# A column maximum over partitions moved from GpSimd to TensorE and VectorE in a fused Fourier, soft-MoE and SwiGLU kernel

## The chip, the core and the metric

The kernel runs on one core of one Trainium2 chip. The metric is the device time of one execution in microseconds; the figure for the kernel before is the median of three runs. A TensorE clock of 1.00 in a profile is 2.4 GHz.

## The reference

The input x has 8 batches of 3072 positions and 256 channels. Three layers follow each other. The first takes a real Fourier transform along the positions, a complex linear map with bias, a soft threshold and the inverse transform. The second is a soft mixture of experts with 8 experts of 4 slots, where the softmax of the dispatch runs over all 8 x 3072 = 24576 tokens and that of the combination over the 32 slots:

```python
logits = x @ phi                                  # 24576 x 32
d = np.exp(logits - logits.max(0, keepdims=True))
d /= d.sum(0, keepdims=True) + 1e-09
slot_input = d.T @ x                              # then two matrices per expert
c = np.exp(logits - logits.max(1, keepdims=True))
c /= c.sum(1, keepdims=True) + 1e-09
x = c @ slot_out
```

The third is an RMS norm with a gated product (silu(xn @ w_gate) * (xn @ w_val)) @ w_out. The change concerns `logits.max(0)`, a maximum per slot over all tokens.

## The kernel before

**Phase 1** (`phase1`) is one main loop (L709) over `u` from 0 to 287: 8 batches, three thirds each, 12 steps `m` per third. A slot in this document is one such step, numbered from the start of the batch in which it runs. In each step `emit_M` issues three matmuls of the complex linear map into one of two psM banks; at fixed steps `emit_A` (first transform stage, L224), `emit_B` (second stage, L261), `emit_T` (transposes through psT or psA, L376) and `emit_L` (logits in the frequency domain, L388) put in their matmuls. The evacuations of what TensorE produced are not issued at once: `post(f, k, rank)` puts them k slots later, at the start of that slot, and lower ranks come first there. L386, for example, is ScalarE's copy that empties the bank of an `emit_T` one slot later (rank -1). `new_t()` hands out the banks psT and psA in turn; `emit_A` can take both of them, and L245 and L247 empty them on ScalarE.

Beside this runs a converter (L131) that turns double-precision weights into fp32 on VectorE, one step in 12 of the 36 slots of a batch, slot 12 among them. L155 is its product; for one of the weights ScalarE's L158 follows it.

**The softmax chain.** `chain(b)` (L407) does the softmax of batch b. For the batches 0 to 6 it is a list of steps, each with the slot of batch b + 1 in which it is issued (the tuples `at`, L611 and L612, the second for the batches 0 to 5; a step with a second number is issued behind the matmuls of its slot). The chain inverts the transform of the logits, which gives 96 partitions x 32 positions x 32 slots (tile `l`). `dmax` (L450) takes the maximum over the 32 positions of a partition into `mx` (96 x 32; `si` in the trace). What is left is the maximum over the 96 partitions. `dpar` (L459) does it on GpSimd with `partition_all_reduce`, which leaves the result on all 128 partitions in `mb`, and `dpre` (L456) does the same with the running maximum of the batch before. `dmn` (L472, or L474 in batch 0) puts `mb` and the old running maximum together on VectorE. `dal` (L483) and `alexp` (L496) make the factor by which older sums are scaled. `dsub` (L487, two halves) and `dexp` (L492) make the dispatch weights, which TensorE uses from slot 23 (`fa`, L536). For the combination `cmax` (L500) takes the row maximum, `csub` (L504) subtracts on VectorE, `cexp` (L508) is an exponential on ScalarE, then `csum` and `cmul` (L518). The result goes to DRAM: for batch 0 in four DMAs on GpSimd's queue (L523), for 1 to 6 in one on SP's queue (L525).

The last batch has a chain of its own, which is issued after the main loop and keeps the all-reduces (`dold` with `dpre`, and `dpar(64)`).

Each engine works through its queue in order. GpSimd's own work in this phase is a subtraction per half `emit_B` (L295), which makes the low part of a high-low pair for the next third. An all-reduce needs another function library on GpSimd than L295, and the queue holds a MODIFY_POOL_CONFIG in front of a change of library.

**Phase 2** (`phase2`) is the experts and the gated product, the rest of the span, and is not touched.

Of the kernel before, what the change touches and what calls it, by code (L numbers as in the profile page):

```python
# [6 lines left out]
F32 = mybir.dt.float32  # L7
# [3 lines left out]
ALU = mybir.AluOpType  # L11
AX = mybir.AxisListType
# [3 lines left out]
NB, N, C = 8, 3072, 256  # L16
# [152 lines left out]
def phase1(tc, x, w_r, w_i, b_r, b_i, phi, t_d, t_bf, t_ci, t_ai, t_af, t_id,  # L169
           ident, s_run, z_run, c_d, cv_args, mid):  # L170
    from contextlib import ExitStack
    nc = tc.nc
# [7 lines left out]
    sm_p, mn_p = P(st_c, "sm", 1), P(st_c, "mn", 2)  # L180
# [13 lines left out]
    mx = mid.si.rearrange("p h s -> p (h s)")  # L194
# [9 lines left out]
    xraw, asb, bounce, bin_t, xq, xs, x0, yy, yts, lfs, mns, mix = ({} for _ in range(12))  # L204
# [3 lines left out]
    def post(f, k=1, rank=1):  # L208

        if clock[0] is None:  # L210
            f()
        else:
            pend.setdefault(clock[0] + k, []).append((rank, len(pend), f))
# [158 lines left out]
    def new_t():  # L372
        turn[0] += 1
        return bank(*((psT, "psT"), (psA, "psA"))[turn[0] % 2])
# [26 lines left out]
    def bank(p, n):  # L401
        return p.tile([128, 512], F32, name=n)
# [4 lines left out]
    def chain(b):  # L407

        S = {}
# [39 lines left out]
            v = S["l", k0].rearrange("p (n s) -> p n s", s=32) if k1 - k0 == 16 else l3(k0, k1)  # L449
            nc.vector.tensor_reduce(out=mx[0:96, o:o + 32], in_=v.rearrange("p n s -> p s n"), axis=AX.X, op=ALU.max)  # L450

        def dpre():
            if b < NB - 1:
                S["mb"] = sm_p.tile([128, 96], F32, name="mb")
            if b:
                nc.gpsimd.partition_all_reduce(out_ap=S["mb"][:, 0:32], in_ap=mns[b - 1], channels=128, reduce_op=ReduceOp.max)  # L456

        def dpar(w):
            nc.gpsimd.partition_all_reduce(out_ap=S["mb"][:, 0:w], in_ap=mx[:, 0:w], channels=128, reduce_op=ReduceOp.max)  # L459

        def dold():
            S["mb"] = sm_p.tile([128, 96], F32, name="mb")
            nc.vector.tensor_copy(out=S["mb"][:, 64:96], in_=mns[b - 1])
            dpre()

        def dmn(w):
            mb = S["mb"][:, 0:32]
            mn = mn_p.tile([128, 32], F32, name="mn")
            if w == 64:
                nc.vector.tensor_reduce(out=mn, in_=S["mb"].rearrange("p (k s) -> p s k", k=3), axis=AX.X, op=ALU.max)  # L470
            elif b:
                nc.vector.tensor_tensor(out=mn, in0=mb, in1=mns[b - 1], op=ALU.max)  # L472
            else:
                nc.vector.tensor_copy(out=mn, in_=mb)  # L474
            mns[b] = S["mn"] = mn
            if w == 32:
                dal()
            S["d"] = ch_p.tile([128, 1024], F32, name="ch")[0:96]

        def dal():  # L480
            if b:
                S["al"] = sm_p.tile([128, 32], F32, name="al")
                nc.vector.tensor_tensor(out=S["al"], in0=mns.pop(b - 1), in1=S["mn"], op=ALU.subtract)  # L483
# [32 lines left out]
        def cmul(eng=nc.gpsimd):  # L516
            S["c"] = ch_p.tile([128, 1024], F32, name="ch")[0:96]
            eng.tensor_tensor(out=S["c"].rearrange("p (n s) -> p n s", s=32), in0=S["e"].rearrange("p (n s) -> p n s", s=32),  # L518
                                    in1=S["sc"].unsqueeze(2).to_broadcast([96, 32, 32]), op=ALU.mult)
            if b == 0:  # L520
                v = c_d[0].rearrange("a b -> (a b)").rearrange("(a t n s) -> a n t s", a=4, t=32, s=32)
                for a in range(4):
                    nc.gpsimd.dma_start(out=v[a], in_=S["c"][24 * a:24 * a + 24].rearrange("n (t s) -> n t s", s=32))  # L523
            elif b < NB - 1:
                nc.sync.dma_start(out=c_d[b], in_=S["c"])  # L525
            else:
                mid.put_c = lambda: nc.sync.dma_start(out=c_d[b], in_=S["c"])
# [54 lines left out]
        def slot(g0, g1, ps):  # L582
            if g0 == 0:
                S["sl"] = ps
            ps = S["sl"]
            for pg in range(g0, g1):
                yt = yts.pop((b, pg))
                for g in range(4):
                    o = 32 * (4 * pg + g)
                    nc.tensor.matmul(out=ps[32 * g:32 * g + 32, 0:256], lhsT=S["D"][:, o:o + 32], rhs=yt[:, g, :],  # L590
                                     start=(pg == 0), stop=(pg == 5))
# [15 lines left out]
        def L(f, *a):  # L607
            return lambda: f(*a)

        if b < NB - 1:  # L610
            at = (12, 6, 9, 10, 10, 10, 13, 13, 11, 15, 14, 18, 19, 20, 16, 16, 25, 30, 22, 22, 26, 26, 29, 30, 32, 33, 34, 35) if b == NB - 2 else \  # L611
                 (12, 7, 8, 9, 9, 10, 13, 13, 15, 16, 13, 14, 19, 20, 15, 16, 18, 28, 23, 23, 26, 27, 31, 28, 28, 33, 34, 35)  # L612
            steps = [(dpre,), (clear,), (L(binv, 0, 24), 1), (L(t1, 0, 32),), (L(ainv, 0), 2), (L(ainv, 1), 2), (L(dmax, 0, 32),),
                     (L(dpar, 32),), (cmax,), (L(csub, nc.vector),), (L(dmn, 32),), (L(dsub, 0, 16),), (L(dsub, 16, 32),),
                     (L(dexp, 0, 32),), (alexp,), (cexp,), (csum,), (L(cmul, nc.vector),), (L(fa, 0, 16), 2),
                     (L(fa, 16, 32), 2), (L(t2, 0, 16),), (L(t2, 16, 32),), (alT,), (L(fb, 0, 12), 1),
                     (L(fb, 12, 24), 1), (L(dT, 0, 6),), (lambda: slot(0, 6, new_t()), 1), (s_up,)]
            return [(a, *e) for a, e in zip(at, steps)]

        def tr(q, ri, k):  # L620
            return lambda: emit_T(b, q, ri, bank(*((psT, "psT"), (psM, "psM"), (psM, "psM"), (psA, "psA"), (psB, "psB"))[k]))

        return [clear, L(binv, 0, 16), tr(0, 0, 1), tr(0, 1, 3), tr(1, 0, 4), lambda: emit_L(b, 2), L(binv, 16, 24),
                L(t1, 0, 16), tr(1, 1, 2), tr(2, 0, 1), L(ainv, 0, (psB, "psB")), L(t1, 16, 32), dold,
                L(ainv, 1, (psA, "psA")), L(dmax, 0, 16), L(lcopy, 0), halved, tr(2, 1, 0), tr(3, 0, 2),
                L(dmax, 16, 32), L(lcopy, 1), L(dpar, 64), tr(3, 1, 1), st_i.close, L(mid.open, 2), tr(4, 0, 0), L(dmn, 64),
                L(dsub, 0, 16), L(dexp, 0, 16), tr(4, 1, 1), L(busy, 2), L(fa, 0, 16, (psB, "psB")), L(dsub, 16, 32),
                L(dexp, 16, 32), dal, L(t2, 0, 16), L(fa, 16, 32, (psA, "psA")), alexp, alT, L(t2, 16, 32),
# [72 lines left out]
    S = 12 * W  # L701
    late, back = {}, {1: [(0, 3)], 8: [(0, 4)], 13: [(0, 5)]}
    for b in range(1, NB):
        for q, k in enumerate((-13, -13, -11, -6, -2, 6) if b > 1 else (-16, -15, -13, -6, -2, 6)):
            back.setdefault(36 * b + k, []).append((b, q))
    last = chain(NB - 1)


    for u in range(S):  # L709
        w, m = divmod(u, 12)  # L710
        b, qq = divmod(w, 3)
        clock[0] = u
        if qq == 0 and m == 0 and 1 <= b:
            for k, f, *pe in chain(b - 1):
                late.setdefault((u + k, pe[0] if pe else 0), []).append(f)
# [13 lines left out]
        if u in (26, 28, 30, 32):  # L729
            p = slice(3 * u - 78, 3 * u - 72)  # L730
# [7 lines left out]
        if w >= 1 and m in (2, 4, 6, 10) and w <= W - 3:  # L738
            k = (2, 4, 6, 10).index(m)
# [7 lines left out]
        at = (3, 5, 7, 9) if w % 3 == 2 else (3, 5, 7, 9)  # L747
        if w + 1 < W and m in at:
            k = at.index(m)
# [552 lines left out]
```

## Time and profile before

| | kernel before |
|---|---|
| median of 3 runs | 1686.51 us (1684.47 to 1688.64) |
| the profiled execution | 1684.44 us, span 1682.7 us |
| TensorE matmul, share of the span | 98% (1648.2 us) |
| VectorE | 77% (1297.2 us) |
| ScalarE | 64% (1073.8 us) |
| GpSimd | 7% (124.5 us, 140 instructions) |
| mean granted TensorE clock | 0.994 |

The span runs from the first to the last instruction of the profiled execution. The busy share of TensorE is modelled from pipelined matmuls, so it says that work was under way, not that it ran at its peak. Where a table of windows shows TensorE less busy than the window is long, it waited; where PEclk is below 1.00, what it did took longer. "Idle before" and the brackets at the end of timeline rows give the wait in front of an instruction and what ended it; "issue" is a wait for nothing that the profile shows.

### The profile page before, as it was taken

The page shows a single profiled execution, that of the slowest core. Times are in us where ns is not written, and L with a number is a line of the kernel's source. Part 1 is how long each engine was busy: PE and PEld are TensorE (multiplying, and loading weights), DVE is VectorE, ACT ScalarE, POOL GpSimd, SP SyncE. Part 2 cuts the span into 40 slices and gives each one's busy share as a digit, 9 for nine tenths or more (in the row PEclk, how much of TensorE's full clock was granted, in tenths as well). Part 3 has the DMA queues.
Part 4 walks back from the last instruction along what each step waited for, and adds up shares of the span by engine and source line. Part 5 has one row for each costly group of instructions (what it writes and reads, how often), then busy time and mean ns, then how long its engine had stood idle before and what let it go on. Part 6 is the DMA issues. An engine that isn't in the chain of part 4 may idle for free.

```text
span 1682.7 us, 27265 instructions
## 1 busy us (share of the span) xinstructions
PE 1648.2 (98%) x10313; PEld 1312.9 (78%) x10313; DVE 1297.2 (77%) x2288; ACT 1073.8 (64%) x2078; POOL 124.5 (7%) x140
## 2 busy tenths in 40 slices
PE   8999999999999999999999999999999999999999
PEld 5667666676676568888888888888888888888887
DVE  3678878778688488878877877877877887887775
ACT  3767666666664376666666666666666666666664
POOL 0112111111111110000000000000000000000000
PEclk9999999999999999999999999999999999999999
DMA  8866666566553931200200110020021021020001
GB/s 307 306 218 194 204 196 209 176 207 215 177 185 123 326 106 39 69 29 26 64 24 24 52 47 26 26 72 26 13 64 35 26 64 35 26 63 13 26 26 38
DMA packets 107619, 172.52 MB, mean 103 GB/s; under 512 B 9248, under 2 KB 70912, under 8 KB 107488
## 3 DMA queue, kind: packets, MB, share of 16 engines
q1 hardware_dynamic: 106912, 169.97, 31.5%
q8 instruction: 81, 1.33, 0.3%
q0 software_dynamic: 432, 0.78, 0.3%
q14 instruction: 50, 0.41, 0.1%
q10 hardware_dynamic: 144, 0.03, 0.0%
HBM read 98.65 MB, written 59.77 MB: 94 GB/s over the span
## 4 chain that ended last, share of the span: by engine, by line
PE 91%; DVE 3%; issue 2%; ACT 2%; DMA 1%; POOL 0%; SPq 0%; ACTq 0%; POOLq 0%
PE po L1185 16%; PE pe L1185 16%; PE psM L319 10%; PE po L1186 8%; PE pe L1186 8%; PE pg L1157 8%; PE pv L1159 8%; PE psB L271 4%; PE psC L237 1%; PE psT L237 1%; PE psA L384 1%; PE psT L384 1%; PE psC L536 1%; PE psC L419 1%; PE psA L590 1%
## 5 line engine op out<-in xcount | busy, mean ns | idle before, releaser
L1163 DVE TENSOR_TENSOR h<-s,pv 128x512 f32<-128x512 f32 x576 | 394.8, 685 | 185.2 <-ACT s L1161 177.0
L1161 ACT ACTIVATE s<-pg 128x512 f32<-128x512 f32 x576 | 345.4, 600 | 296.9 <-PE pg L1157 295.5
L1185 PE MATMUL po<-wo,hh 128*128 128x512 f32 x1152 | 428.6, 396 | 0.0
L1185 PE MATMUL pe<-wo,hh 128*128 128x512 f32 x1152 | 423.9, 392 | 0.0
L107 DVE TENSOR_TENSOR hl<-h,hh 128x512 fp32r<-128x512 f32 x572 | 400.2, 700 | 0.1
L106 ACT ACTIVATE hh<-h 128x512 fp32r<-128x512 f32 x576 | 360.6, 626 | 1.4 <-DVE h L1163 1.2
L1186 PE MATMUL po<-wo,hl 128*128 128x256 f32 x1152 | 322.5, 280 | 0.0
L1186 PE MATMUL pe<-wo,hl 128*128 128x256 f32 x1152 | 322.0, 280 | 0.0
L1185 PEld LDWEIGHTS po<-wo,hh 128*128 128x128 f32 x1152 | 216.3, 188 | 50.9
L1185 PEld LDWEIGHTS pe<-wo,hh 128*128 128x128 f32 x1152 | 216.4, 188 | 49.7
L1186 PEld LDWEIGHTS pe<-wo,hl 128*128 128x128 f32 x1152 | 215.9, 187 | 22.9
L1157 PE MATMUL pg<-cq,gst 128*128 128x512 f32 x576 | 227.8, 396 | 0.7 <-ACT cq L1090 0.7
L1159 PE MATMUL pv<-cq,gst 128*128 128x512 f32 x576 | 227.0, 394 | 0.3 <-DVE h L1163 0.2
L1186 PEld LDWEIGHTS po<-wo,hl 128*128 128x128 f32 x1152 | 216.3, 188 | 2.7
L319 PE MATMUL psM<-xq,wh 128*128 128x512 f32 x384 | 169.8, 452 | 0.3 <-DVE yy L332 0.3
L1157 PEld LDWEIGHTS pg<-cq,gst 128*128 128x128 f32 x576 | 108.5, 188 | 25.1 <-ACT cq L1090 1.1
L271 PEld LDWEIGHTS psB<-bf,bin 128*128 128x128 f32 x752 | 98.8, 195 | 24.9 <-issue 13.9
L1159 PEld LDWEIGHTS pv<-cq,gst 128*128 128x128 f32 x576 | 109.0, 189 | 2.2 <-DVE h L1163 1.7
L295 POOL TENSOR_TENSOR xs<-xt,xs 128x256 fp32r<-128x256 f32 x92 | 78.2, 851 | 391.9 <-ACT xs L294 367.2
L271 PE MATMUL psB<-bf,bin 128*128 128x128 f32 x752 | 102.8, 281 | 4.3 <-DMA bin<-bounce 2.5
L319 PEld LDWEIGHTS psM<-xq,wh 128*128 128x128 f32 x384 | 73.7, 192 | 34.8 <-issue 24.2
L335 ACT ACTIVATE r<-yy,b_lo 128x512 f32<-128x512 f32 (+1 forms) x92 | 66.2, 720 | 27.5 <-DVE yy L338 27.3
(311 smaller groups left out, 1873.6 us busy)
## 6 DMA issues: line engine op xcount, KB each, us to landing
xraw<-in_x_dram SPq DMA_DIRECT2D x52, 512.0 KB, 4.9
bin<-bounce SPq DMA_DIRECT2D x48, 512.0 KB, 5.4
out_dram<-o SPq DMA_DIRECT2D x45, 512.0 KB, 2.9
bounce<-xraw SPq DMA_DIRECT2D x104, 192.0 KB, 3.2
ex<-in_moe_w_dram SPq DMA_DIRECT2D x16, 1024.0 KB, 8.4
yt<-in_x_dram SPq DMA_DIRECT2D x12, 512.0 KB, 8.0
cq<-chi SPq DMA_DIRECT2D x56, 96.0 KB, 2.1
cq<-clo SPq DMA_DIRECT2D x56, 96.0 KB, 2.1
```

Source lines behind the costliest of these rows:

```text
L106: nc.scalar.activation(out=hi, in_=src, func=AF.Copy)
L107: (lo_eng or nc.vector).tensor_tensor(out=lo, in0=src, in1=hi.bitcast(F32), op=ALU.subtract)
L271: nc.tensor.matmul(out=ps[:, 128 * j:128 * j + 128], lhsT=t[:, j, 128 * h:128 * h + 128], rhs=bf[:, 4 * q + j, :], start=True, stop=True)
L295: nc.gpsimd.tensor_tensor(out=s_lo, in0=xsum, in1=s_hi.bitcast(F32), op=ALU.subtract)
L319: nc.tensor.matmul(out=ps, lhsT=w[k - 1][:, h, cs], rhs=X, start=(h == 0 and n == 0), stop=(h == 1 and n == 2))
L335: nc.scalar.activation(out=r[:, o:], in_=Y, func=AF.Relu, bias=b_lo[:, ri, ch:ch + 1])
L1157: nc.tensor.matmul(out=pg, lhsT=gst[:, 128 * fb:128 * fb + 128], rhs=v, start=True, stop=True)
L1159: nc.tensor.matmul(out=pv, lhsT=gst[:, 1536 + 128 * fb:1536 + 128 * fb + 128], rhs=v, start=True, stop=True)
L1161: nc.scalar.activation(out=s, in_=pg, func=AF.Silu)
L1163: nc.vector.tensor_tensor(out=h, in0=s, in1=pv, op=ALU.mult)
L1185: nc.tensor.matmul(out=ps, lhsT=hh[:, ts], rhs=wo[:, fb].rearrange("p k c -> p (k c)"), start=(fb == 0), stop=False)
L1186: nc.tensor.matmul(out=ps[:, 0:256], lhsT=hl[:, ts], rhs=wo[:, fb, 0], start=False, stop=(fb == 11))
```

## The change

The change replaces `dpre` and `dpar(32)` by three steps. `mT`, behind the matmuls of slot 13, transposes `mx` on TensorE into 32 partitions x 96 in psT or psA. `mred`, at the start of slot 14, reduces this on VectorE to one maximum per slot and spreads it along 128 columns. `mB`, behind the matmuls of slot 14, multiplies the spread tile with the identity, which leaves the maximum of each slot on all 128 partitions of a psT or psA bank. `dmn` follows at the start of slot 15 and reads that bank. The slots of several steps are set anew: `dmax` goes from 13 to 12, `alexp` from 15 to 16 (16 stays for batch 6), `cexp` from 16 to 17, the first `dsub` from 14 to 15. In batch 6 the row maximum goes from 11 to 12, `csub` from 15 to 14 and the first `dsub` from 18 to 15. The four DMAs of batch 0 are posted 1, 3, 5 and 7 slots behind slot 28 in place of all at once. The last batch's chain computes as before.

```diff
@@ -449,25 +449,34 @@
             v = S["l", k0].rearrange("p (n s) -> p n s", s=32) if k1 - k0 == 16 else l3(k0, k1)
             nc.vector.tensor_reduce(out=mx[0:96, o:o + 32], in_=v.rearrange("p n s -> p s n"), axis=AX.X, op=ALU.max)
 
-        def dpre():
-            if b < NB - 1:
-                S["mb"] = sm_p.tile([128, 96], F32, name="mb")
-            if b:
-                nc.gpsimd.partition_all_reduce(out_ap=S["mb"][:, 0:32], in_ap=mns[b - 1], channels=128, reduce_op=ReduceOp.max)
+        def mT():
+            S["mt"] = new_t()
+            nc.tensor.transpose(out=S["mt"][0:32, 0:96], in_=mx[0:96, 0:32], identity=ident[0:96, 0:96])
+            post(mred, 1, -1)
+
+        def mred():
+            S["mb"] = sm_p.tile([128, 128], F32, name="mb")
+            nc.vector.tensor_reduce(out=mx[0:32, 32:33], in_=S["mt"][0:32, 0:96], axis=AX.X, op=ALU.max)
+            nc.vector.tensor_scalar(out=S["mb"][0:32], in0=ident[0:32], scalar1=0.0, scalar2=mx[0:32, 32:33], op0=ALU.mult, op1=ALU.add)
+
+        def mB():
+            S["mt"] = new_t()
+            nc.tensor.matmul(out=S["mt"][:, 0:32], lhsT=S["mb"][0:32], rhs=ident[0:32, 0:32], start=True, stop=True)
+            post(lambda: dmn(32), 1, -1)
 
         def dpar(w):
             nc.gpsimd.partition_all_reduce(out_ap=S["mb"][:, 0:w], in_ap=mx[:, 0:w], channels=128, reduce_op=ReduceOp.max)
 
         def dold():
-            S["mb"] = sm_p.tile([128, 96], F32, name="mb")
+            S["mb"] = sm_p.tile([128, 128], F32, name="mb")
             nc.vector.tensor_copy(out=S["mb"][:, 64:96], in_=mns[b - 1])
-            dpre()
+            nc.gpsimd.partition_all_reduce(out_ap=S["mb"][:, 0:32], in_ap=mns[b - 1], channels=128, reduce_op=ReduceOp.max)
 
         def dmn(w):
-            mb = S["mb"][:, 0:32]
+            mb = S["mt"][:, 0:32] if w == 32 else None
             mn = mn_p.tile([128, 32], F32, name="mn")
             if w == 64:
-                nc.vector.tensor_reduce(out=mn, in_=S["mb"].rearrange("p (k s) -> p s k", k=3), axis=AX.X, op=ALU.max)
+                nc.vector.tensor_reduce(out=mn, in_=S["mb"][:, 0:96].rearrange("p (k s) -> p s k", k=3), axis=AX.X, op=ALU.max)
             elif b:
                 nc.vector.tensor_tensor(out=mn, in0=mb, in1=mns[b - 1], op=ALU.max)
             else:
@@ -520,7 +529,7 @@
             if b == 0:
                 v = c_d[0].rearrange("a b -> (a b)").rearrange("(a t n s) -> a n t s", a=4, t=32, s=32)
                 for a in range(4):
-                    nc.gpsimd.dma_start(out=v[a], in_=S["c"][24 * a:24 * a + 24].rearrange("n (t s) -> n t s", s=32))
+                    post(lambda a=a: nc.gpsimd.dma_start(out=v[a], in_=S["c"][24 * a:24 * a + 24].rearrange("n (t s) -> n t s", s=32)), 2 * a + 1)
             elif b < NB - 1:
                 nc.sync.dma_start(out=c_d[b], in_=S["c"])
             else:
@@ -608,10 +617,10 @@
             return lambda: f(*a)
 
         if b < NB - 1:
-            at = (12, 6, 9, 10, 10, 10, 13, 13, 11, 15, 14, 18, 19, 20, 16, 16, 25, 30, 22, 22, 26, 26, 29, 30, 32, 33, 34, 35) if b == NB - 2 else \
-                 (12, 7, 8, 9, 9, 10, 13, 13, 15, 16, 13, 14, 19, 20, 15, 16, 18, 28, 23, 23, 26, 27, 31, 28, 28, 33, 34, 35)
-            steps = [(dpre,), (clear,), (L(binv, 0, 24), 1), (L(t1, 0, 32),), (L(ainv, 0), 2), (L(ainv, 1), 2), (L(dmax, 0, 32),),
-                     (L(dpar, 32),), (cmax,), (L(csub, nc.vector),), (L(dmn, 32),), (L(dsub, 0, 16),), (L(dsub, 16, 32),),
+            at = (6, 9, 10, 10, 10, 12, 13, 14, 12, 14, 15, 19, 20, 16, 17, 25, 30, 22, 22, 26, 26, 29, 30, 32, 33, 34, 35) if b == NB - 2 else \
+                 (7, 8, 9, 9, 10, 12, 13, 14, 15, 16, 15, 19, 20, 16, 17, 18, 28, 23, 23, 26, 27, 31, 28, 28, 33, 34, 35)
+            steps = [(clear,), (L(binv, 0, 24), 1), (L(t1, 0, 32),), (L(ainv, 0), 2), (L(ainv, 1), 2), (L(dmax, 0, 32),),
+                     (mT, 2), (mB, 2), (cmax,), (L(csub, nc.vector),), (L(dsub, 0, 16),), (L(dsub, 16, 32),),
                      (L(dexp, 0, 32),), (alexp,), (cexp,), (csum,), (L(cmul, nc.vector),), (L(fa, 0, 16), 2),
                      (L(fa, 16, 32), 2), (L(t2, 0, 16),), (L(t2, 16, 32),), (alT,), (L(fb, 0, 12), 1),
                      (L(fb, 12, 24), 1), (L(dT, 0, 6),), (lambda: slot(0, 6, new_t()), 1), (s_up,)]
```

## Rows read from the trace of the kernel before

**Rows 1.** The page's chain of waits, shares of the span by engine.

```profile
PE 91%; DVE 3%; issue 2%; ACT 2%; DMA 1%; POOL 0%; SPq 0%; ACTq 0%; POOLq 0%
```

**Rows 2.** Waits, 110 to 560 us: who for whom, us in total, times, longest.

```profile
POOL mb L456 <- issue: 49.5, 7, 11.2
DVE mn L472 <- POOL mb L459: 24.5, 6, 4.8
DVE mn L474 <- POOL mb L459: 3.6, 1, 3.6
```

**Rows 3.** Tile mb, GpSimd's all-reduces: count, ns min/median/max, first and last start.

```profile
L459 POOL PARTITION_ALL_REDUCE mb<-si x8: 432/433/523, 119.3 to 557.6; - x8
L456 POOL PARTITION_ALL_REDUCE mb<-mn x7: 452/453/456, 185.0 to 546.1; - x7
```

**Rows 4.** Sum of six windows between the chains: length, then busy by engine.

```profile
sum 323.00, PE 322.89 PEld 233.03 DVE 249.64 ACT 216.20 POOL 59.09; mean PE 53.82 PEld 38.84 DVE 41.61 ACT 36.03 POOL 9.85
```

**Rows 5.** Windows behind the seven chains: length; busy PE, PEld, DVE, ACT, POOL; PEclk, DMA, GB/s.

```profile
120.00:130.00 10.00, 8.02 (x61) 5.12 (x58) 9.86 (x17) 6.02 (x11) 0.84 (x2) 1.00 0.48 147
186.00:201.00 15.00, 12.60 (x72) 8.42 (x68) 13.46 (x23) 10.13 (x19) 1.45 (x2) 0.77 0.50 152
254.00:264.00 10.00, 7.71 (x59) 4.00 (x57) 8.38 (x15) 5.64 (x12) 1.61 (x3) 1.00 0.40 132
322.00:330.00 8.00, 5.10 (x42) 2.88 (x42) 7.16 (x13) 4.36 (x9) 0.60 (x2) 1.00 0.35 124
386.00:402.00 16.00, 12.97 (x83) 8.62 (x82) 12.02 (x20) 8.49 (x18) 3.09 (x4) 0.89 0.44 118
458.00:470.00 12.00, 8.87 (x54) 5.38 (x55) 11.26 (x19) 7.41 (x15) 1.88 (x4) 0.86 0.32 102
514.00:534.00 20.00, 16.24 (x90) 11.30 (x89) 15.52 (x24) 10.71 (x24) 4.51 (x6) 1.00 0.01 2
```

**Rows 6.** Timeline of batch 1's chain: start, us, engine, line; waits in brackets.

```profile
177.82 0.69 DVE L332 TENSOR_TENSOR yy<-psM,s 128x511 f32<-128x511 f32 x1 [0.28 <-PE psM L319]
178.43 0.96 DVE L155 SCALAR_TENSOR_TENSOR cve<-cve,cva 128x512 f32<-128x512 f32 x1
179.97 2.03 DVE L450 TENSOR_REDUCE si<-ch 96x32 f32<-96x1024 f32 x1
181.80 0.60 PE L384 MATMUL psT<-ident,yy 128*128 128x128 f32 x4
186.02 0.19 DVE L472 TENSOR_TENSOR mn<-mb,mn 128x32 f32<-128x32 f32 x1 [4.02 <-POOL mb L459]
190.40 1.06 ACT L508 ACTIVATE ch<-ch 96x1024 f32<-96x1024 f32 x1 [2.46 <-DVE ch L504]
191.36 0.58 ACT L386 ACTIVATE yt<-psA 128x512 f32<-128x512 f32 x1
191.99 0.66 PE L384 MATMUL psA<-ident,yy 128*128 128x128 f32 x4 [1.70 <-ACT yt L386]
```

**Rows 7.** Groups, 110 to 560 us: busy us, mean ns of one, idle before.

```profile
L384 PE MATMUL psA<-ident,yy 128*128 128x128 f32 x152 | 22.9, 273 | 5.1 <-ACT yt L386 5.1
L470 DVE TENSOR_REDUCE mn<-mb 128x32 f32<-128x96 f32 x1 | 0.3, 262 | 0.7 <-POOL mb L459 0.7
L513 DVE TENSOR_SCALAR sc<-sc 96x32 f32<-96x32 f32 x7 | 1.3, 183 | 0.2
```

**Rows 8.** Timeline of ScalarE at slot 12 of batch 5's chain.

```profile
451.28 0.63 ACT L158 ACTIVATE cvr<-cve 128x512 fp32r<-128x512 f32 x1 [0.78 <-DVE cve L155]
452.29 0.59 ACT L247 ACTIVATE xraw<-psA 128x512 f32<-128x512 f32 x1
```

**Rows 9.** Timeline at slots 12 to 14 of batch 6's chain.

```profile
514.07 1.22 DVE L500 TENSOR_REDUCE mc<-ch 96x32 f32<-96x1024 f32 x1 [1.55 <-ACT ch L439]
515.93 0.50 PE L319 MATMUL psM<-xs,wh 128*128 128x512 f32 x1 [0.23 <-DVE yy L332]
```

**Rows 10.** Timeline of GpSimd, batch 0's DMAs.

```profile
142.56 3.75 POOL L523 DMA_DIRECT2D c_d<-ch  x4 [7.22 <-DVE ch L518]
```

## The prediction

> **What bounds the kernel now.** I read the chain of waits, the list of waits for 110 to 560 us, windows around each chain, and last the timeline of one batch. In the chain TensorE holds 91% of the span and VectorE 3% [rows 1]: only time in which TensorE waits or runs slowly can be won. The change touches the seven softmax chains of batches 0 to 6, so the stretch to read is 110 to 560 us. Its list of waits names the maximum over partitions twice [rows 2]: VectorE sits idle for 24.5 us (six times) and 3.6 us (once) until GpSimd's all-reduce (L459) has landed, some 4 us per chain. The same list says why it is late: GpSimd itself stands still 49.5 us in seven times before L456, the first all-reduce of a chain, with nothing to wait for but the pool configuration in front of it [rows 2].
>
> Does that hold TensorE? Two tables of windows answer. Between the chains TensorE is busy 322.89 of 323 us [rows 4]. In the seven stretches behind the all-reduces it is busy less than their length: 1.98, 2.40, 2.29, 2.90, 3.03, 3.13 and 3.76 us are missing, 19.5 us in all [rows 5]. In three of them the clock also fell to the lower level of 1.2 GHz for some microseconds after TensorE had been idle: the means 0.77 over 15 us, 0.89 over 16 and 0.86 over 12 are 3.4 + 1.8 + 1.7 = 6.9 us. So **26.4 us** stand against these chains, and next to nothing against anything else in this phase.
>
> How a wait of VectorE reaches TensorE is in the timeline of batch 1 [rows 6]. VectorE ends the maximum per partition (L450) at 182.0 and then has nothing for 4.02 us, because the next entry of its queue is the copy of the all-reduce (L472). The rest of the chain slides back, so ScalarE waits 2.46 us for the subtraction L504 with the exponential L508 at the head of its queue; behind that exponential stands L386, which empties the bank that TensorE's next transpose (L384) wants. TensorE gets it at 191.99, 1.70 us late. The transpose is that of slot 18: the stall reaches TensorE four slots after it began on VectorE.
>
> **The change, part by part.** A slot is one turn of the main loop, counted from the start of the chain's host batch.
>
> *All-reduces out.* Seven of the L459 and six of the L456 go, with their configurations; the last batch keeps one of each. VectorE's 28.1 us of waiting goes, and with it the 26.4 us of TensorE, if nothing as late takes its place. ScalarE's exponential also moves from slot 16 to 17 in every chain, where the L386 posted for slot 17 comes before it: the blockade of 191 us is broken twice. The other small moves (first subtraction 14 to 15, alpha's exponential 15 to 16) have slack until the exponential of slot 20 and cost nothing; if that slack were gone, TensorE would wait at slot 23.
>
> *Work for TensorE.* Per chain one transpose and one 32-column product, 14 instructions. The nearest row is L384: four 128-column transposes in 0.60 us, 0.15 each [rows 6]; alone one takes 273 ns [rows 7]. Bounds 2.1 and 3.8 us. I take **2.1**, since the matmuls behind do not depend on them and stream on. The Trainium skill (TensorE: Matmul & The Clock Gate, Single matmul latency) says that an isolated matmul cannot hide its fill and drain while a stream of them costs little more than its columns; reading the new pair as isolated, the term would be 3.8 and the forecast 1.7 us later.
>
> *Work for VectorE.* A reduction of 96 columns (row L470: 262 ns) and a 128-column scalar operation of about 0.2 us [rows 7], in place of 4 us of idleness: free, except where TensorE waits for them, next.
>
> *Two new waits in TensorE's in-order queue.* At the end of slot 13 the transpose waits for the partition maximum; at the end of slot 14 the product waits for reduction and scalar operation, with slot 15's matmuls behind it. Batch 1 shows it [rows 6]: the maximum now stands in slot 12, behind L332 (177.82) and ahead of the converter's L155, so it runs from 178.5 to 180.5. Then L155 and the L338 behind it (1.54 us from the start of L155 to that of the maximum in the rows, about 1.65 with the end of the second) are done about 182.2, reduction and scalar operation about 182.75. TensorE's slot-13 matmuls end about 181.1 (slot 14 has three more of 0.23 before its transposes at 181.80): no wait for the transpose. The product stands ready about 182.3 and waits **0.5 us**. Batches 0 to 4 look alike: 5 x 0.5 = 2.5 (bounds 0 and 1 each, since VectorE's order is fixed and its durations are rows).
> Batch 5 differs: its converter step of slot 12 puts ScalarE's L158 behind L155 [rows 8]. L155 slides 2 us back behind the maximum, L158 from 451.28 to 453.4, and the emptying of the two banks (L245, then L247, today at 452.29) to about 454.6 and 455.1; the new transpose, ready at 453.4, needs one of them: **1.7 us** instead of 0.5 (bounds 1.2 and 2.5).
> Batch 6 differs too: its step of slot 12 holds the partition maximum and then the row maximum L500. The data arrive at 514.07 [rows 9], L332 goes first, the maximum ends about 516.6, the row maximum 517.8, L338 518.4, reduction and scalar operation 518.9. TensorE, which today starts slot 14 at 515.93 after a short wait, reaches the transpose about 515.45, waits 1.2, reaches the product 0.9 later and waits 1.4: **2.6 us** (bounds 1.5 and 4), most of what this chain loses today.
> VectorE gets two waits of its own: the reduction for the transpose and the maximum with the old one for the product. Queued behind them are L338, the row maximum, the subtractions and, from slot 17, the emptying of psB. TensorE's product is done about 0.4 us before VectorE has finished L338, so neither should hold.
>
> *What is left of the old stalls.* Between nothing and all of it. The row nearest is the stretch between the chains: 0.11 us of idleness in 323 [rows 4]. VectorE is tight behind the chain, though (13.46 of 15 us [rows 5]), so I take one short wait such as the 0.23 in rows 9 per chain: **1.8 us**.
>
> *Four DMAs of batch 0.* On GpSimd's queue they run together from 142.56, 0.93 us each [rows 10]; spread over slots 29, 31, 33 and 35 each stands before at most one of GpSimd's 0.74 us subtractions, which GpSimd's idleness covers; TensorE was busy throughout that stretch [rows 4]. Zero; without cover at most 0.9 us each. Their buffer is wanted again a batch later. SP's queue is not passed by anything. The last chain's library load now is the only one of the phase: its first all-reduce starts at 546.1 after the longest of the standstills, 11.2 us, and the second, on which the chain waits, at 557.6 [rows 2, 3]: 11 us of margin, zero.
>
> **Sum:** 26.4 - 2.1 - 2.5 - 1.7 - 2.6 - 1.8 = 15.7 us. The profiled execution took 1684.44 us; 1668.7 follows. The median shown is 2.07 us above it, so I forecast **1671 us**. Phase 2 starts from positions in the program, not from a clock, so it moves up as a whole. (A measurement of this kernel tells 0.3%, 5.1 us, from no change.)
>
> **Rivals.**
> *Better than the sum, 0.12.* VectorE's queue lets every product through without a wait and batches 5 and 6 lose nothing new. Only TensorE's 2.1 stay: 24.3 won, 1662 us. For it: 0.11 us of idleness between the chains. Against: VectorE's order, read from the rows, puts 3.7 us ahead of the reduction.
> *The clock does not come back, 0.15.* The pauses at the two new waits are followed by a fall to 1.2 GHz, as those of three stretches are today [rows 5]; then 6.9 is not won: 15.7 - 6.9 = 8.8, 1678 us. Against: only batch 6 has pauses of that order left.
> *The stall moves, 0.08.* VectorE is dense in slots 14 to 20, and half of the 26.4 comes back as waits for psB and psM: 13.2 less the other costs of 2.1 + 2.5 + 1.7 + 2.6 = 8.9 is 4.3 us won, 1682 us, about no change. Against: the same VectorE, with the 4 us of idleness, is what has to catch up today.
> *TensorE waits instead of VectorE, 0.05.* The place is the product of slot 14, in an in-order queue. VectorE today may run behind because ScalarE feeds it; but if VectorE reaches the reduction late in every chain, each microsecond there is paid by TensorE in full, where today it has other work until the transpose of 191.99. From (26.4 - 2.1)/7 = 3.5 us of waiting per chain on it is a loss; at 5 us, 35 + 2.1 - 26.4 gives 10.7 us, 1697 us. For it: batch 6 already comes to 2.6. Against: in batches 0 to 4 VectorE's work ahead (3.7 us) is as long as TensorE's.
>
> **Numbers.** Forecast 0.60 and the four rivals 0.12, 0.15, 0.08, 0.05. The forecast's own bounds (1.7 for TensorE's work, 2.5 for the waits of batches 0 to 4, 0.8 and 1.4 for 5 and 6, up or down, and 1.8 down) give 1665 to 1677; with the clock's case and the better one the range is 1662 to 1681, and the last two rivals stay outside. Faster by over 0.3% is below 1681.4: 0.60 + 0.12 + 0.15 and a little of the moved stall, 0.88; within 0.3%: 0.07; slower 0.05.
>
> **What would show it.** Right: no VectorE wait on GpSimd before 550 us; in batch 1 the partition maximum directly behind L332, L386 of slot 17 ahead of the exponential, TensorE waiting about 0.5 us at the product; the same seven stretches short of 5 to 9 us in all instead of 19.5; granted clock 1.00 there. Wrong: a row of TensorE's product with several microseconds of idleness in front in every chain, the clock still falling, or VectorE's waits for the product of the size of the old ones.

## The result and the profile after

The changed kernel takes **1665.15 us** (median of 4 runs, 1661.11 to 1667.52), beside 1685.7 us for the kernel before in the same session: ratio **0.9873**, 95% interval 0.9849 to 0.9897. It is 20 us faster. The profiled execution took 1664.77 us, its span 1663.0 us, the mean granted clock 0.998 (0.994 before).

Lines behind the change have new numbers. In the chain: L454 is the new transpose, L459 and L460 the reduction and the scalar operation behind it, L464 the product with the identity, L481 the maximum with the old one. L509, L513 and L517 are the row maximum, its subtraction and the exponential (L500, L504, L508 before); L473 and L468 are the two all-reduces that the last chain keeps.

First the page's chain of waits, shares of the span by engine:

```profile
PE 95%; DMA 2%; DVE 1%; ACT 1%; issue 0%; SPq 0%; POOL 0%; ACTq 0%
```

Against [rows 1] TensorE has 95% instead of 91% and VectorE 1% instead of 3%.

Next the list of waits for 110 to 560 us, those lines that name GpSimd's maximum and TensorE's waits at the new instructions (who for whom, us in total, times, longest):

```profile
POOL mb L473 <- issue: 10.6, 1, 10.6
...
PE psT L464 <- DVE mb L460: 1.2, 1, 1.2
...
PE psA L454 <- DVE si L450: 1.1, 1, 1.1
...
PE psT L454 <- ACT xraw L245: 0.8, 1, 0.8
...
DVE mn L479 <- POOL mb L468: 0.7, 1, 0.7
```

VectorE's two lines of [rows 2], 24.5 and 3.6 us, are gone; the 0.7 us that it waits for an all-reduce belong to the last chain, as before [rows 7]. One of GpSimd's seven standstills is left, 10.6 us, in the last chain. At the new instructions TensorE waits three times: at the transpose in two chains of seven, at the product in one.

The last chain's margin, in GpSimd's timeline:

```profile
525.47 0.69 POOL L473 PARTITION_ALL_REDUCE mb<-mn  x1 [10.63 <-issue]
537.51 0.52 POOL L468 PARTITION_ALL_REDUCE mb<-si  x1 [11.35 <-DVE si L450]
```

The standstill ended 12 us before the all-reduce on which the chain waits.

Where TensorE still lost time: windows of the stretch of the seven chains (length; busy PE, PEld, DVE, ACT, POOL; clock, DMA, GB/s). The four hold losses; the last line is the sum of the five stretches between and behind them, from 112 to 186, 194 to 394, 398 to 438, 442 to 494 and 502 to 530 us, up to the last chain.

```profile
186.00:194.00 8.00, 7.05 (x49) 5.19 (x44) 6.90 (x12) 5.66 (x12) 1.42 (x2) 1.00 0.59 193
394.00:398.00 4.00, 3.43 (x30) 2.48 (x32) 3.73 (x6) 2.51 (x5) 0.00 (x0) 1.00 0.95 312
438.00:442.00 4.00, 3.16 (x19) 2.34 (x18) 1.97 (x5) 4.00 (x8) 0.00 (x0) 1.00 0.43 123
494.00:502.00 8.00, 5.71 (x24) 3.60 (x23) 6.02 (x9) 3.37 (x7) 0.74 (x1) 1.00 0.00 1
...
sum 394.00, PE 394.00 PEld 280.15 DVE 327.36 ACT 266.20 POOL 68.53; mean PE 78.80 PEld 56.03 DVE 65.47 ACT 53.24 POOL 13.71
```

The four windows miss 0.95 + 0.57 + 0.84 + 2.29 = 4.65 us of TensorE, where [rows 5] missed 19.5. The clock is 1.00 in every one, where three of [rows 5] had 0.77 to 0.89. Everywhere else TensorE is busy all the time. What ended each pause stands in brackets in TensorE's timeline (start, us, engine, line):

```profile
190.10 1.09 PE L237 MATMUL psC<-xraw,dt 48*64 48x512 f32 x8 [0.95 <-DMA xraw<-in_x_dram]
395.21 1.13 PE L271 MATMUL psB<-bf,bin 128*128 128x128 f32 x8 [0.57 <-DMA bin<-bounce]
439.15 0.26 PE L454 MATMUL psT<-ident,si 96*32 96x96 f32 x1 [0.84 <-ACT xraw L245]
498.44 0.24 PE L454 MATMUL psA<-ident,si 96*32 96x96 f32 x1 [1.09 <-DVE si L450]
500.60 0.40 PE L464 MATMUL psT<-ident,mb 32*128 32x32 f32 x2 [1.19 <-DVE mb L460]
```

Two are loads, of input and of the bounced tile, for which TensorE did not wait in this stretch before. They change from one execution to the next: in a second profile of the same kernel they are 0.47 and 0.82 us, the second at another place. The other three stand at the new instructions, in the chains of batches 5 and 6.

Batch 1's chain, the part that answers to [rows 6]:

```profile
176.25 0.69 DVE L332 TENSOR_TENSOR yy<-psM,s 128x511 f32<-128x511 f32 x1 [0.27 <-PE psM L319]
176.53 0.73 POOL L295 TENSOR_TENSOR xs<-xt,xs 128x256 fp32r<-128x256 f32 x1 [4.22 <-ACT xs L294]
176.85 1.88 DVE L450 TENSOR_REDUCE si<-ch 96x32 f32<-96x1024 f32 x1
178.66 0.67 DVE L155 SCALAR_TENSOR_TENSOR cve<-cve,cva 128x512 f32<-128x512 f32 x1
...
179.53 0.25 PE L454 MATMUL psT<-ident,si 96*32 96x96 f32 x1
179.92 0.24 DVE L459 TENSOR_REDUCE si<-psT 32x1 f32<-32x96 f32 x1
180.19 0.27 DVE L460 TENSOR_SCALAR mb<-ident,si 32x128 f32<-32x128 f32 x1
180.88 0.40 PE L464 MATMUL psT<-ident,mb 32*128 32x32 f32 x2
181.45 0.18 DVE L481 TENSOR_TENSOR mn<-psT,mn 128x32 f32<-128x32 f32 x1
184.24 0.60 ACT L386 ACTIVATE yt<-psA 128x512 f32<-128x512 f32 x1 [0.16 <-PE psA L384]
187.47 1.04 ACT L517 ACTIVATE ch<-ch 96x1024 f32<-96x1024 f32 x1
188.55 0.60 PE L384 MATMUL psA<-ident,yy 128*128 128x128 f32 x4
```

L481 runs with no wait 4.60 us after the start of L450 (181.45 - 176.85); its counterpart L472 came 6.05 us after it (186.02 - 179.97), 4.02 of them waiting. L386 of slot 17 now comes before the exponential L517, and the transposes of slot 18 (188.55) have no bracket: the 1.70 us of [rows 6] are gone. The product, L464, has none either.

**Where the 20 us lie.** Both kernels reach the first matmul of L237 in slot 12 of batch 0's chain at the same time, 112.66 us (112.63 before). The first expert matmul starts at 551.33 us, at 571.37 before; from there to the end it is 1111.7 us after and 1111.3 before. So 20.0 us come from the stretch of the chains and none from the second phase. The first matmul of L237 in slot 12 of batch 5's chain stands at 435.46, at 450.27 before, 14.8 us earlier; the other 5.2 are won behind it.

### The profile page after: what moved, and what is told of

The parts are those of the page before. It is cut to its first block, busy times and chain, and to the rows that moved or that the text cites. A ratio compares the mean times of both kernels' runs of the same rounds, so it can differ in the third digit from the quotient of the medians.

```text
span 1663.0 us, 27274 instructions
## 1 busy us (share of the span) xinstructions
PE 1645.6 (99%) x10334; PEld 1313.7 (79%) x10334; DVE 1299.1 (78%) x2302; ACT 1074.6 (65%) x2078; POOL 119.8 (7%) x127
## 4 chain that ended last, share of the span: by engine, by line
PE 95%; DMA 2%; DVE 1%; ACT 1%; issue 0%; SPq 0%; POOL 0%; ACTq 0%
PE po L1194 16%; PE pe L1194 16%; PE psM L319 11%; PE po L1195 8%; PE pe L1195 8%; PE pg L1166 8%; PE pv L1168 8%; PE psB L271 5%; PE psC L237 2%; PE psT L237 1%; PE psT L384 1%; PE psA L384 1%; DMA xraw<-in_x_dram 1%; PE psA L396 1%; PE psC L419 1%; PE psA L599 1%
## 5 line engine op out<-in xcount | busy, mean ns | idle before, releaser
L319 PE MATMUL psM<-xq,wh 128*128 128x512 f32 x384 | 167.6, 446 | 0.0
L271 PEld LDWEIGHTS psB<-bf,bin 128*128 128x128 f32 x752 | 96.7, 191 | 20.8 <-issue 12.6
L295 POOL TENSOR_TENSOR xs<-xt,xs 128x256 fp32r<-128x256 f32 x92 | 79.6, 866 | 421.9 <-ACT xs L294 421.8
L271 PE MATMUL psB<-bf,bin 128*128 128x128 f32 x752 | 100.6, 277 | 1.0 <-DMA bin<-bounce 1.0
L319 PEld LDWEIGHTS psM<-xq,wh 128*128 128x128 f32 x384 | 72.5, 189 | 32.7 <-issue 22.6
```

What stands on the lines that cost most here:

```text
L271: nc.tensor.matmul(out=ps[:, 128 * j:128 * j + 128], lhsT=t[:, j, 128 * h:128 * h + 128], rhs=bf[:, 4 * q + j, :], start=True, stop=True)
L295: nc.gpsimd.tensor_tensor(out=s_lo, in0=xsum, in1=s_hi.bitcast(F32), op=ALU.subtract)
L319: nc.tensor.matmul(out=ps, lhsT=w[k - 1][:, h, cs], rhs=X, start=(h == 0 and n == 0), stop=(h == 1 and n == 2))
```

## The experiments

My theory: the cause is the place in VectorE's queue at which the all-reduce is read, before GpSimd has changed its library; TensorE's share comes through that wait. The rivals: GpSimd's standstill itself, the exponential's slot, the DMAs, and the place of the partition maximum. Each kernel was timed beside the kernel before in its session (1684.95 us in the first four, 1686.65 in the next four, 1684.25 in the last two).

**One part alone: the four DMAs of batch 0**, in the kernel before.

```
-                    nc.gpsimd.dma_start(out=v[a], in_=S["c"][24 * a:24 * a + 24]...)
+                    post(lambda a=a: nc.gpsimd.dma_start(out=v[a], ...), 2 * a + 1)
```

> The kernel before, with only the four DMAs of batch 0 spread over slots 29 to 35. My theory (the gain is VectorE's wait for the all-reduce): no change, within 0.3% of the kernel before, since TensorE was busy throughout the stretch of the four DMAs. Rival (the spread DMAs free GpSimd and carry part of the gain): 2 us or more faster.

1686.5 us (10 runs), ratio 1.0006 (0.9991 to 1.002). No gain or loss is seen from the DMAs.

**The all-reduces kept, only read later.** In the kernel before the maximum's step (dmn) goes from slot 13 or 14 to 17, the first subtraction and alpha's exponential to 18; nothing is removed.

```
- (12, 7, 8, 9, 9, 10, 13, 13, 15, 16, 13, 14, 19, 20, 15, 16, 18, ...)
+ (12, 7, 8, 9, 9, 10, 13, 13, 15, 16, 17, 18, 19, 20, 18, 16, 18, ...)
```

> The kernel before, all-reduces on GpSimd kept, but the step that reads them on VectorE moved from slot 13 or 14 to slot 17, the first subtraction to 18, alpha's exponential to 18. If it is the place of VectorE's wait that cost the time, 24.5 + 3.6 us of waiting shrink below 5 us and the time comes 12 to 20 us below the kernel before. Rival 1 (the library changes on GpSimd cost through its own queue, L295 late and the banks behind it): VectorE's wait goes and less than 8 us are won. Rival 2 (the wait only moves): VectorE waits as long at slot 17, no gain.

1664.5 us (1662.46 to 1666.95), ratio 0.9884 (0.9859 to 0.9908): the whole gain of the change, a little over the 12 to 20 us expected, with every all-reduce in place. Its list of waits, 110 to 560 us:

```profile
ACT xt L282 <- POOL xs L295: 13.4, 7, 4.3
...
DVE mn L472 <- POOL mb L459: 0.3, 1, 0.3
```

VectorE's 24.5 us are 0.3, and the 3.6 us of L474 are gone. That settles it: the wait was a matter of where in VectorE's queue the read stood, not of who computes the maximum. The first line is the price that is left on this way: L295, which needs the other library, now holds ScalarE (2.4 us, once, in the kernel before). In batch 6 it costs (windows, then the timeline there):

```profile
110.00:502.00 392.00, 390.72 (x3184) 277.27 (x3183) 326.83 (x577) 273.19 (x539) 73.37 (x90) 1.00 0.63 200
...
506.00:510.00 4.00, 2.45 (x3) 1.17 (x4) 2.88 (x6) 3.12 (x7) 1.82 (x3) 0.57 0.00 0
```

```profile
505.43 1.40 POOL L295 TENSOR_TENSOR xs<-xt,xs 128x256 fp32r<-128x256 f32 x2 [6.79 <-issue]
506.18 0.38 ACT L282 ACTIVATE xt<-psB 128x256 f32<-128x256 f32 x1 [4.29 <-POOL xs L295]
507.55 3.78 PE L536 MATMUL psC<-ch,af 96*128 96x512 f32 x4 [3.48 <-ACT ch L492]
```

GpSimd stands still 6.79 us on the way back from the all-reduces. ScalarE's L282 waits for it, the exponential L492 stands behind L282, and TensorE pauses 3.48 us for that exponential; the clock falls to 0.57. In the 392 us before that only 1.28 us are missing.

**The standstill put back into the changed kernel.** One all-reduce per chain of batches 1 to 6, whose result nobody reads.

```
         def mT():
+            if b:
+                nc.gpsimd.partition_all_reduce(out_ap=mid.ri, in_ap=mns[b - 1], channels=128, reduce_op=ReduceOp.max)
```

> The changed kernel plus, in the chains of batches 1 to 6, one all-reduce on GpSimd of the old running maximum at slot 13, whose result nothing reads: the library changes and the standstill of GpSimd are back, VectorE's wait is not. My theory: under 3 us slower than the changed kernel (batch 6, where L295 is wanted soon, about 1.5 us). Rival (GpSimd's standstill itself is what TensorE felt): 10 us or more slower.

1667.02 us (1664.98 to 1668.12), ratio 0.9892 (0.9872 to 0.9912), 1.9 us above the changed kernel's median and inside each other's intervals. Its windows in batch 6:

```profile
498.00:502.00 4.00, 2.06 (x7) 1.51 (x8) 3.64 (x7) 1.20 (x2) 0.00 (x0) 0.79 0.00 0
502.00:506.00 4.00, 4.00 (x14) 3.03 (x12) 2.32 (x4) 1.59 (x4) 0.45 (x1) 0.50 0.00 0
506.00:510.00 4.00, 4.00 (x32) 2.78 (x32) 1.96 (x4) 1.46 (x3) 0.00 (x0) 0.86 0.00 0
```

Here the clock fell (0.79, 0.50, 0.86 make 0.8 + 2.0 + 0.6 = 3.4 us), as it didn't in the profile of the changed kernel. The fall can't be put down to the unread all-reduces alone: in the second profile of the changed kernel (below) the clock fell in batch 6 too, to 0.84 from 498 to 502 us and 0.73 from 502 to 506, 1.7 us. Six standstills for which nobody waits cost about 2 us (3 by the two ratios), hardly more than the scatter: the standstill by itself is not the cause.

**The partition maximum one slot later** (12 to 13) in the changed kernel, so that TensorE's transpose comes right behind it.

```
- (7, 8, 9, 9, 10, 12, 13, 14, 15, 16, 15, 19, 20, 16, 17, ...)
+ (7, 8, 9, 9, 10, 13, 13, 14, 15, 16, 15, 19, 20, 16, 17, ...)
```

> The changed kernel with the maximum per partition issued in slot 13 as before, so one slot later than in the change, everything else kept. TensorE reaches the transpose at the end of slot 13 and waits for the maximum. From the rows of batch 1 the maximum would end about 1.3 us later than now (behind L155 and L338), 0.9 us after TensorE is ready, and the product then waits too for VectorE's two small operations: 1 to 2 us per chain, 7 to 14 us slower than the changed kernel in all. If TensorE's queue has slack at that place instead: under 3 us.

1670.74 us (1668.82 to 1673.79), ratio 0.9917 (0.9894 to 0.9941): 5.6 us above the changed kernel's median in its own session, 7.4 us by the two ratios: at the lower end of the 7 to 14 that I expected. Groups, 110 to 530 us (busy, mean ns of one, idle before):

```profile
L454 PE MATMUL psA<-ident,si 96*32 96x96 f32 x4 | 1.0, 262 | 5.3 <-DVE si L450 5.3
L454 PE MATMUL psT<-ident,si 96*32 96x96 f32 x3 | 0.7, 243 | 2.4 <-DVE si L450 1.6 <-ACT xraw L243 0.8
```

TensorE waits 7.7 us at the seven transposes, where the changed kernel waits 0.84 + 1.09: in six chains 0.8 to 0.9 us, in batch 6 2.8. Behind that last wait the clock also fell (0.78, 0.50 and 0.86 in the three windows of 4 us from 502), another 3.4 us. That is the mechanism of the rival "TensorE waits instead", in six chains about a quarter of its break-even of 3.5 us per chain. The move from slot 13 to 12 is what keeps it out.

**The exponential's slot**, first put back to 16 in the changed kernel, then moved alone to 17 in the kernel before.

```
- (7, 8, 9, 9, 10, 12, 13, 14, 15, 16, 15, 19, 20, 16, 17, 18, ...)
+ (7, 8, 9, 9, 10, 12, 13, 14, 15, 16, 15, 19, 20, 16, 16, 18, ...)
```

> The changed kernel with ScalarE's exponential back in slot 16, ahead of L386 of slot 17, as before the change. My theory (L386 was held only because the subtraction L504 came late): the subtraction now ends 3.5 us before TensorE wants the bank, so L386 is still in time and the time stays within 2 us of the changed kernel. Rival (the order of exponential and L386 carries the gain): 8 us or more slower than the changed kernel.

1665.57 us (1662.77 to 1666.32), ratio 0.987 (0.985 to 0.989): no difference. Once nothing is late, the order of L386 and the exponential makes no difference that these runs show.

```
- (12, 7, 8, 9, 9, 10, 13, 13, 15, 16, 13, 14, 19, 20, 15, 16, 18, ...)
+ (12, 7, 8, 9, 9, 10, 13, 13, 15, 16, 13, 14, 19, 20, 15, 17, 18, ...)
```

> The kernel before with only the exponential moved from slot 16 to 17, so that L386 goes first although VectorE still waits for the all-reduce. Theory: the pauses of about 1.7 us before L384 of slot 18 go in batches 0 to 5, with the clock falls that followed them; what stays are the 0.3 to 1.2 us in front of L396 and batch 6: 8 to 15 us faster than the kernel before, 5 us or more slower than the changed kernel. Rival (VectorE's lateness reaches TensorE by other ways at once): under 5 us faster.

1680.93 us (10 runs, 1677.69 to 1682.16), ratio 0.9961 (0.995 to 0.9972): 5.7 us, below the 8 to 15 that I expected. One window over the whole stretch, of this kernel and then of the kernel before:

```profile
110.00:530.00 420.00, 402.65 (x3213) 282.75 (x3212) 334.65 (x589) 276.10 (x550) 75.31 (x93) 1.00 0.60 188
```

```profile
110.00:530.00 420.00, 401.74 (x3203) 283.44 (x3200) 330.02 (x581) 273.37 (x543) 72.65 (x92) 0.98 0.59 187
```

TensorE is idle almost as much as before (17.4 us, 18.3 before), but the clock is 1.00 instead of 0.98: what it won is clock. That is no accident of one profile: the mean granted clock is 0.997 to 0.999 in its ten runs and 0.990 to 0.995 in the 15 of the kernel before. The move alone broke the long pause into pieces behind other lines, as in its timeline of TensorE in batch 0's chain:

```profile
129.96 1.13 PE L271 MATMUL psB<-bf,bin 128*128 128x128 f32 x8 [0.36 <-ACT r L335]
131.92 0.50 PE L319 MATMUL psM<-xq,wh 128*128 128x512 f32 x1 [0.84 <-DVE yy L332]
```

VectorE still waits 24.4 us in L472 for the all-reduces; its lateness reaches TensorE over the emptying of other banks. So the exponential at the head of ScalarE's queue was the path the stall took, not its source.

**Batch 6's row maximum behind the partition maximum's reduction**, in the changed kernel: row maximum from slot 12 to 15, its subtraction from 14 to 16.

```
- (6, 9, 10, 10, 10, 12, 13, 14, 12, 14, 15, 19, 20, ...)
+ (6, 9, 10, 10, 10, 12, 13, 14, 15, 16, 15, 19, 20, ...)
```

> The changed kernel with the row maximum of batch 6 moved from slot 12 to 15 and its subtraction from 14 to 16, as in the other batches. Theory: in batch 6 the reduction behind the transpose no longer stands behind L509's 1.2 us, so TensorE's 1.1 us before the transpose stay (the data arrive late) and the 1.2 us before the product go: 1 to 2 us faster than the changed kernel, and no fall of the clock there. Rival: VectorE then is late at slot 16 to 19 and the same time is lost there, no change.

1662.98 us (1660.89 to 1668.38), ratio 0.9867 (0.9845 to 0.9889). The wait at the product goes:

```profile
494.00:498.00 4.00, 2.98 (x11) 1.69 (x9) 2.59 (x3) 1.96 (x4) 0.74 (x1) 1.00 0.00 0
498.00:502.00 4.00, 3.86 (x24) 2.83 (x28) 3.60 (x8) 2.47 (x5) 0.00 (x0) 1.00 0.00 2
```

1.16 us are missing instead of 2.29. A microsecond is less than the runs scatter; the total shows no more than that it is not slower.

**A mixed kernel.** Batches 0 to 5 as in the experiment with the late read (GpSimd's all-reduces, the read in slot 17), batch 6, where GpSimd's way back was dear, over TensorE with the late row maximum, and the four DMAs spread.

```
-            mb = S["mt"][:, 0:32] if w == 32 else None
+            mb = S["mb" if b < NB - 2 else "mt"][:, 0:32] if w == 32 else None
...
+            if b < NB - 2:
+                steps[5:8] = [(L(dmax, 0, 32),), (L(dpar, 32),), (cmax,), (L(csub, nc.vector),), (L(dmn, 32),)]
+                del steps[10:12]
+                steps.insert(0, (dpre,))
```

> Batches 0 to 5 with the all-reduce on GpSimd and its result read late (slot 17, as in e3_late_mn), batch 6 by TensorE as in the change, with its row maximum in slot 15 and the DMAs spread. Theory: in batches 0 to 5 nothing is left but 1.2 us of pauses and no new work on TensorE, in batch 6 the pauses of 3.5 us and the fall of the clock of e3_late_mn shrink to about 1 us: 3 to 6 us faster than the changed kernel, about 1660 us. Rival: the library changes on GpSimd cost in batch 6 as well through its later all-reduces, same as the changed kernel.

1661.46 us (1660.01 to 1662.22), ratio 0.9848 (0.9828 to 0.9867): the fastest so far, but its interval overlaps the changed kernel's from another session. So both ran again in one session.

> The changed kernel, unaltered, so that it and the mixed kernel are timed in the same session on the same chip. Every theory expects its 1665 us (1661 to 1668) again, ratio to before 0.987. If it comes out at 1662 or below, the gain seen for the mixed kernel belonged to the session.

1665.65 us (1664.82 to 1667.94), ratio 0.9891 (0.987 to 0.9913).

> The mixed kernel (batches 0 to 5 with GpSimd's all-reduces read late, batch 6 over TensorE), unaltered, beside the changed kernel. If TensorE's new work costs the 1.75 us net that the balance of the changed kernel gives, and batch 6's later row maximum saves about 1 us, it stays 2 to 4 us below the changed kernel: 1661 to 1663 us, ratio to before 0.985. If both are bound by the same rest, the two medians lie within 1 us of each other.

1661.54 us (1659.58 to 1662.84), ratio 0.9863 (0.9842 to 0.9884). The two kernels' runs don't overlap: the mixed kernel is 4.1 us faster, 0.25%. Between the first matmul of L237 in slot 12 of batch 0's chain and the experts it takes 436.6 and 436.8 us in its two profiles, against 438.7 and 440.6 in the two of the change. So 2 to 4 us of the difference lie in the stretch of the chains. Which of its parts gives how much, the late row maximum or the matmuls saved in six chains, was not taken apart by a run. At the 0.64 us per chain that the next section reads from the rows, the matmuls saved are 6 x 0.64 = 3.8 us, an estimate, and the greater part; the 1.75 us for all seven in the expectation above were too few.

## Why the prediction was right

It forecast 1671 us, 1662 to 1681, faster; it is 1665. The sign and the cause hold; the sum was 4 us too careful (15.7 against 19.7 by the two profiled executions, 1684.44 and 1664.77). That it came out so near is in part luck: the gain and the price of the new work were both put too low, by 2.7 and 2.4 us, and nearly cancel. What is left of the difference are the waits, put too high. By its own steps:

- **"All-reduces out", 26.4 us.** Right in source, too small in size. With the wait gone, 4.65 us of idleness stand where 19.5 were, and none of the 6.9 us of the lower clock (1.7 in batch 6 of the second profile). The late-read kernel shows that it was this wait. The size follows from what was won and what was paid, by the items below: 20.0 + 4.5 + 0.84 + 2.28 + 1.52 = 29.1 us. The brackets in front of rows show less than a pause takes: in an unbroken stream L319's rows start 0.23 us apart and last 0.39, so the idle time of a row is counted from 0.16 us behind the point where it could have started. With 21 pauses in the seven stretches that is up to 3.4 us, an estimate that covers the 2.7. The remark that ScalarE's blockade is "broken twice" was wrong in its weight: put back to slot 16 the exponential costs nothing that the runs show, so without the wait its slot does not matter.
- **"Work for TensorE", 2.1 us (bounds 2.1 and 3.8).** This term was mis-sized: the new work took about 4.5 us, its waits not counted. Batch 1's chain shows it, from TensorE's first matmul of slot 13 to L271 in slot 15, before and then after:

```profile
180.29 0.51 PE L319 MATMUL psM<-xs,wh 128*128 128x512 f32 x1
...
182.93 1.05 PE L271 MATMUL psB<-bf,bin 128*128 128x128 f32 x8
```

```profile
178.72 0.51 PE L319 MATMUL psM<-xs,wh 128*128 128x512 f32 x1
...
182.01 1.05 PE L271 MATMUL psB<-bf,bin 128*128 128x128 f32 x8
```

The way is 2.64 us long before and 3.29 after, with no bracket in either. In batch 0 it is 2.64 and 3.28, and in the late-read kernel, which has no new work, 2.64. So a chain pays 0.64 us, seven some 4.5 (an estimate for batches 5 and 6, where the waits stand in the same place). The count was wrong: in fp32 the product is two matmuls, each with its own weight load, so that 21 and not 14 matmuls were added. The price of each was too low as well: the two rows last 0.25 and 0.40 us, where the forecast took 0.15 each, from four transposes in a run. The Trainium skill (TensorE: Matmul & The Clock Gate, Step-by-step: what each phase is for) says that a single isolated matmul can't hide its drain. Read so, the term was 3.8 for the 14 instructions that the forecast counted; the 4.5 of this case for 21 matmuls speak for that reading and against 2.1.
- **"Two new waits", batches 0 to 4, 2.5 us.** This step failed: TensorE did not wait at the product there at all. The 3.7 us from L450's start to the reduction were taken from durations of before; they were 3.07 (176.85 to 179.92). L155 took 0.67 instead of 0.96 (below), L450 1.88 instead of 2.03. TensorE came to the product 4.63 us after the start of L332, as forecast (4.5). The lower bound, 0, is what came.
- **Batch 5, 1.7 us.** The mechanism is right: the transpose waits for L245, which stands behind L158, and that waits for L155, as ScalarE's timeline shows. The term was 0.84, below its bound of 1.2; here too L155 took 0.67 us.

```profile
437.98 0.63 ACT L158 ACTIVATE cvr<-cve 128x512 fp32r<-128x512 f32 x1 [2.30 <-DVE cve L155]
438.51 0.58 ACT L245 ACTIVATE xraw<-psT 128x512 f32<-128x512 f32 x1
```

- **Batch 6, 2.6 us.** 1.09 at the transpose and 1.19 at the product, 2.28 in all against 1.2 and 1.4. The experiment with the row maximum moved confirms the cause of the second.
- **"What is left of the old stalls", 1.8 us.** 1.52 us were left, but elsewhere: two late loads in place of one short wait per chain. The size was met by accident.
- **Four DMAs, zero, and the last library load, zero.** Both hold within what the runs tell, the first by its own experiment (1.0006), the second with 12 us of margin where 11 were forecast.

Of the **rivals**, *better than the sum* comes nearest, with 1662: batches 0 to 4 let every product through, but 5 and 6 do lose. *The clock does not come back* is not seen in the first profile of the change and is seen in a small part in the second, 1.7 us in batch 6; the kernels with the unread all-reduce and with the late read lose clock at the same place. *The stall moves* is what the exponential alone did, not the change. *TensorE waits instead* is a question of one slot, as the maximum in slot 13 shows.

## What to carry to other kernels

Before an operation is replaced because its consumer waits for it, look at where the consumer stands in its queue: here reading the old result three or four slots later won as much as computing it elsewhere. New work for the bounding engine brings few waits as long as what it waits for is issued a slot earlier, but it is paid for all the same: price a lone small matmul by what a lone one takes, not by its share of a run of four, and count how many matmuls the product becomes. Durations of VectorE taken from a trace hold for the neighbours they had there, and moving an instruction changes the neighbours.

## What the runs showed of the hardware

**L155's duration follows what GpSimd does beside it.** L155 in the chain's slot 12 took 0.95 to 0.96 us in five chains of the kernel before, each time with 0.40 us of GpSimd's L295 beside it; its other 11 executions, with L295 elsewhere, took 0.66 to 0.69. In the changed kernel the maximum has pushed it behind L295 and all 16 are short; with the maximum in slot 13 it is back beside L295, and five are 0.95 to 0.96 again. By tile and line (ns min, median, max), of before, of the change and of the kernel with the maximum in slot 13:

```profile
L155 DVE SCALAR_TENSOR_TENSOR cve<-cve,cva x16: 657/684/959, 112.7 to 484.9; 128x512 f32<-128x512 f32 x16
```

```profile
L155 DVE SCALAR_TENSOR_TENSOR cve<-cve,cva x16: 653/682/686, 114.6 to 466.6; 128x512 f32<-128x512 f32 x16
```

```profile
L155 DVE SCALAR_TENSOR_TENSOR cve<-cve,cva x16: 661/685/959, 112.5 to 470.9; 128x512 f32<-128x512 f32 x16
```

It is not so for every instruction of VectorE, and it depends on which of the two starts first. In the kernel before L338, which reads nothing from PSUM, took 0.82 to 1.21 us in seven executions with 0.27 to 0.66 us of an L295 beside it that had started earlier; where L338 started first it kept its 0.73 to 0.75 us in 18 of 19, and L295 took 0.99 to 1.28 instead of 0.73. L332, which reads a bank of PSUM, took 0.65 to 0.69 us in every one of its 78 executions in that stretch, many with L295 beside it all the time. What the two engines share was not tested.

**A small fp32 product is two matmuls.** Tile mb of the changed kernel, one of the two banks:

```profile
L464 PEld LDWEIGHTS psT<-ident,mb x8: 181/182/184, 180.9 to 500.7; 32*128 32x128 f32 x8
L464 PE MATMUL psT<-ident,mb x8: 271/282/292, 180.9 to 500.7; 32*128 32x32 f32 x8
```

Four chains, eight of each. The transpose L454 is one matmul of 0.25 us.

**GpSimd's change of library costs on the way back too:** 6.79 us before L295 in the late-read kernel, with ScalarE waiting for 4.29 us. The Trainium skill (GPSIMD Engine Reference, 2.1 Instruction dispatch) names about 6 us for the first call of a freshly loaded kernel; this row agrees in size, and the last chain's 10.6 us do not. Why those are longer stays open.
